# Spectral products of a long convolution: from paired half-array matmuls with the complex sum on VectorE to full 128x128 matmuls with the complex sum inside the inverse transform

## The chip, the cores and the metric

One core of a Trainium2 chip runs the whole program. The metric is the device time of one execution in microseconds (us); I quote medians. Engines are called as the profile calls them: PE is TensorE's matmul, PEld its weight load, DVE is VectorE, ACT is ScalarE, POOL is GpSimd, SP issues DMAs. The "granted clock" of a profile is the share of full TensorE clock that was granted.

## The reference, cut to what matters

There are two independent heads on 2048 positions and 576 channels. Head A is a dilated sliding-window attention. Head B multiplies shifted keys with values and convolves the result with a filter as long as the sequence; only this convolution is changed.

```python
def _B_ref(q, k, v, shift_k, ssm_k, ssm_D):
    ...                                        # kv = (k * 4-tap filter) * v
    kv_f = rfft(kv padded to 2S, float32)
    kf_f = rfft(ssm_k padded to 2S, float32)
    y_f = kv_f * kf_f                          # complex product per frequency and channel
    y = irfft(y_f)[:S].astype(bfloat16)
    y = y + kv * ssm_D
    return q * y
```

## The kernel before

The transform is split in two stages. Stage 1 writes its result to DRAM (`Dx` for the signal, `Dk` for the filter). Stage 2 is done in 8 steps i (two halves of the channels, four groups of 8 "h" columns): a **kernel transform** `kh_step(i)`, a **signal transform** `g_spec(i)`, the **product** `g_prod(i)` and the **inverse** `g_inv(i)`. These steps are interleaved with the attention's weighted sum over values, the **pv steps** tp = 0 to 7: `pv_mul` (DVE, tile `P`), `pv_sum` (PE, evicted by ACT into `xT`) and `pv_out`. Last, `y_step` does the final stage of the inverse.

```python
    def s2(Wt, g, dst, scale):                 # 64 columns per matmul: two h side by side in the array
        for prl in range(4):
            ps = psb()                         # 2 buffers of two PSUM banks
            for im in range(2):
                for hp in range(2):
                    nc.tensor.matmul(ps[64 * hp:64 * hp + 64, im, 0:HD],          # HD = 288
                                     W2[:, im, 8 * g + 2 * prl + hp].rearrange("p l f -> p (l f)"),
                                     Wt[:, 2 * prl + hp, :], start=True, stop=True, tile_position=(0, 64 * hp))
            nc.scalar.activation(dst[:, :, prl, :], ps[:, :, 0:HD], ACT.Copy, scale=scale)

    def g_prod(i):                             # 4 DVE instructions per step
        ...
        pin(nc.vector.tensor_tensor(m1[:], Xc[:], Kc[:, 0].unsqueeze(1).to_broadcast([128, 2, 4, HD]), ALU.mult))
        pin(nc.vector.tensor_tensor(m2, Xc[:], Kc[:, 1].unsqueeze(1).to_broadcast([128, 2, 4, HD]), ALU.mult))
        pin(nc.vector.tensor_tensor(m1[:, 0], m1[:, 0], m2[:, 1], ALU.subtract))
        pin(nc.vector.tensor_tensor(m1[:, 1], m1[:, 1], m2[:, 0], ALU.add))

    def g_inv(i):                              # 64 rows per matmul: two h above each other in the array
        ...
            for zi in range(2):
                for hp in range(2):
                    nc.tensor.matmul(ps[:, hp, 0:HD], IAt[64 * hp:64 * hp + 64, zi, 4 * g + prl, :],
                                     m1[64 * hp:64 * hp + 64, zi, prl, :], start=(zi == 0), stop=(zi == 1),
                                     tile_position=(64 * hp, 0))
            nc.scalar.activation(Y[:, 2 * prl:2 * prl + 2, :], ps[:, :, 0:HD], ACT.Copy)
        ...
    # k = kernel transform, g = signal step, y = last stage, per pv step tp
    plan = [(("k4", "g0"), ("k5", "g1")), (("k6", "g2"),), (("k7", "g3"), ("g4",)), (("g5",), ("y0",)),
            (("g6",), ("y1",), ("y2",)), (("g7",), ("y3",)), (("y4",), ("y5",)), (("y6",), ("y7",))]
    g_spec(0)
    for tp in range(8):
        pv_mul(tp)
        ...                                    # kh_step of the plan
        for n, i in enumerate(ng):
            if i + 1 < 8:
                g_spec(i + 1)
            if n == 0:
                pv_sum(tp)
            g_prod(i)
            if n == 0 and tp > 0:
                pv_out(tp - 1)
            g_inv(i)
        ...
```

`pin` keeps the DVE instructions of products and of `P` in program order. The order of everything else in an engine's queue is chosen when the program is built.

## Time and profile before

269.2 us (269.17, 269.21 and 271.84). The first part of the page gives busy time, share of the span and number of instructions of each engine:

```profile
span 268.5 us, 5519 instructions
PE 235.0 (88%) x2326; PEld 138.5 (52%) x2326; DVE 202.6 (75%) x216; ACT 163.4 (61%) x236; POOL 23.4 (9%) x59
```

The groups of instructions of the kernel before that the change touches. The columns are line, engine, operation, output <- inputs, shapes and count; then busy us and mean ns of one; then idle time just before them and what ended it:

```profile
L526 PE MATMUL psB<-Wt,W 128*64 128x288 bf16 x256 | 29.2, 311 | 7.1 <-ACT Xc L529 3.0
L529 ACT ACTIVATE Xc<-psB 128x576 bf16<-128x576 f32 x32 | 20.1, 649 | 3.4 <-PE psB L526 3.0
L529 ACT ACTIVATE Kc<-psB 128x576 bf16<-128x576 f32 x32 | 20.0, 650 | 2.2 <-PE psB L526 1.7
L568 DVE TENSOR_TENSOR m<-Xc,Kc 128x2304 bf16<-128x2304 bf16 x8 | 10.8, 1356 | 8.3 <-ACT Xc L529 7.3
L650 PEld LDWEIGHTS <-P 128*128 128x128 bf16 x512 | 30.0, 98 | 14.0 <-issue 8.6
```

The last of these is the weight load of the pv sums. It stood 8.6 us in "issue", that is, waiting for nothing that the profile shows. The timeline of the kernel before shows where (start us, length us, engine, line, what, how many, idle before):

```profile
187.48 0.44 PE L526 MATMUL psB<-Wt,W 128*64 128x288 bf16 x4
187.84 0.23 PEld L650 LDWEIGHTS <-P 128*128 128x128 bf16 x4 [0.23 <-issue]
187.84 0.40 PE L650 MATMUL psA<-ident,P 128*128 128x128 bf16 x4
188.17 0.14 PEld L526 LDWEIGHTS <-W 128*64 128x64 bf16 x4
188.17 0.44 PE L526 MATMUL psB<-Wt,W 128*64 128x288 bf16 x4
...
205.75 0.66 PE L581 MATMUL psB<-m,IAt 64*128 64x288 bf16 x8
...
210.71 0.42 PE L581 MATMUL psB<-m,IAt 64*128 64x288 bf16 x4
...
211.32 2.12 PE L666 MATMUL psA<-wv,xT 128*128 128x288 bf16 x16 [0.20 <-ACT xT L652]
```

Two things are to be read here. Each return from the half array (128\*64) to the full one (128\*128) shows an idle of 0.23 us ahead of the weight load. And the half-array matmuls run in pairs: 8 of L581 take 0.66 us and 4 take 0.42 us, so four more cost 0.24 us, 60 ns each. 16 full ones of the same 288 columns (L666) take 2.12 us, 130 ns each.

### The profile page before, as it was taken

The page shows a single profiled execution, that of the slowest core. Times are in us where ns is not written, and L with a number is a line of the kernel's source. Part 1 is how long each engine was busy: PE and PEld are TensorE (multiplying, and loading weights), DVE is VectorE, ACT ScalarE, POOL GpSimd, SP SyncE. Part 2 cuts the span into 40 slices and gives each one's busy share as a digit, 9 for nine tenths or more (in the row PEclk, how much of TensorE's full clock was granted, in tenths as well). Part 3 has the DMA queues.
Part 4 walks back from the last instruction along what each step waited for, and adds up shares of the span by engine and source line. Part 5 has one row for each costly group of instructions (what it writes and reads, how often), then busy time and mean ns, then how long its engine had stood idle before and what let it go on. Part 6 is the DMA issues. An engine that isn't in the chain of part 4 may idle for free.

```text
span 268.5 us, 5519 instructions
## 1 busy us (share of the span) xinstructions
PE 235.0 (88%) x2326; PEld 138.5 (52%) x2326; DVE 202.6 (75%) x216; ACT 163.4 (61%) x236; POOL 23.4 (9%) x59
## 2 busy tenths in 40 slices
PE   2999969999899999998997578898979998978793
PEld 2236344434366555464653247555645676847671
DVE  2599997999645576589986999879397668799431
ACT  2454448777736565858568895888867666251131
POOL 8200000000000000000068101000000010201200
PEclk9999999999999999999999989999997999999997
DMA  7996594785144352577276676464517576837945
GB/s 256 320 386 227 165 386 134 242 264 175 47 133 125 109 166 88 148 218 272 69 216 172 215 200 197 130 217 137 181 46 254 188 234 186 247 116 242 347 132 176
DMA packets 42544, 52.11 MB, mean 194 GB/s; under 512 B 2284, under 2 KB 35708, under 8 KB 42520
## 3 DMA queue, kind: packets, MB, share of 16 engines
q1 hardware_dynamic: 41190, 48.52, 55.7%
q0 software_dynamic: 1328, 3.25, 4.4%
q8 instruction: 18, 0.29, 0.5%
q14 instruction: 6, 0.05, 0.0%
q10 hardware_dynamic: 2, 0.00, 0.0%
HBM read 30.82 MB, written 18.87 MB: 185 GB/s over the span
## 4 chain that ended last, share of the span: by engine, by line
PE 56%; DVE 22%; ACT 11%; issue 4%; DMA 4%; POOL 2%; SPq 0%; ACTq 0%; DVEq 0%; POOLq 0%
PE psA L278 7%; PE psA L469 6%; PE psA L650 6%; PE psA L261 6%; PE psB L336 6%; PE psB L526 5%; DVE P L640 5%; PE psB L419 3%; PE psA L666 3%; DVE tA L375 3%; DMA Wt<-Dy 3%; DVE tB L370 2%; DVE m L568 2%; DVE sk L569 2%; ACT Xc L529 2%
## 5 line engine op out<-in xcount | busy, mean ns | idle before, releaser
L341 ACT ACTIVATE vst<-psB 128x768 bf16<-128x768 f32 x48 | 37.0, 812 | 12.7 <-PE psB L336 11.3
L466 DVE TENSOR_TENSOR wide<-q,k 128x2048 bf16<-128x2048 bf16 x32 | 38.9, 1228 | 7.4 <-PE psA L469 7.3
L640 DVE TENSOR_TENSOR P<-vX,vt 128x4608 bf16<-128x4608 bf16 x16 | 40.5, 2554 | 2.9 <-PE psA L656 2.8
L650 PE MATMUL psA<-ident,P 128*128 128x128 bf16 x512 | 37.7, 221 | 3.6 <-DVE P L640 2.9
L650 PEld LDWEIGHTS <-P 128*128 128x128 bf16 x512 | 30.0, 98 | 14.0 <-issue 8.6
L526 PE MATMUL psB<-Wt,W 128*64 128x288 bf16 x256 | 29.2, 311 | 7.1 <-ACT Xc L529 3.0
L278 PE MATMUL psA<-xT,wq 128*128 128x512 bf16 x128 | 34.4, 404 | 0.7 <-ACT xT L181 0.7
L469 PE MATMUL psA<-wide,Eh 128*32 128x256 bf16 x256 | 21.7, 400 | 1.1 <-ACT vX L266 1.1
L526 PEld LDWEIGHTS <-W 128*64 128x64 bf16 x256 | 12.9, 112 | 18.2 <-issue 14.9
L529 ACT ACTIVATE Xc<-psB 128x576 bf16<-128x576 f32 x32 | 20.1, 649 | 3.4 <-PE psB L526 3.0
L690 DVE TENSOR_TENSOR m<-psB,tA 128x576 bf16<-128x576 f32 x16 | 11.7, 755 | 13.8 <-PE psB L689 10.0
L584 ACT ACTIVATE tB<-psB 128x576 bf16<-128x576 f32 x32 | 19.4, 658 | 4.1 <-PE psB L581 3.0
L529 ACT ACTIVATE Kc<-psB 128x576 bf16<-128x576 f32 x32 | 20.0, 650 | 2.2 <-PE psB L526 1.7
L278 PEld LDWEIGHTS <-wq 128*128 128x128 bf16 x128 | 12.1, 101 | 16.2 <-issue 6.1
L261 PE MATMUL psA<-wv,xT 128*128 128x288 bf16 x128 | 19.9, 292 | 0.6 <-ACT vX L266 0.6
L629 POOL DMA_DIRECT2D wv<-in_A_wo_dram x18 | 8.9, 499 | 128.5 <-PE psA L261 127.3
L652 ACT ACTIVATE xT<-psA 128x1024 bf16<-128x1024 f32 x8 | 8.2, 1023 | 19.4 <-PE psA L650 19.4
L673 ACT ACTIVATE stageA<-psA 128x576 bf16<-128x576 f32 x16 | 9.5, 648 | 16.8 <-PE psA L670 11.6
L666 PE MATMUL psA<-wv,xT 128*128 128x288 bf16 x128 | 17.1, 286 | 2.0 <-ACT xT L652 2.0
L266 ACT ACTIVATE vX<-psA 128x576 bf16<-128x576 f32 x16 | 10.4, 650 | 12.4 <-PE psA L264 12.4
L261 PEld LDWEIGHTS <-xT 128*128 128x128 bf16 x128 | 15.6, 146 | 4.5 <-issue 3.6
L568 DVE TENSOR_TENSOR m<-Xc,Kc 128x2304 bf16<-128x2304 bf16 x8 | 10.8, 1356 | 8.3 <-ACT Xc L529 7.3
(126 smaller groups left out, 341.7 us busy)
## 6 DMA issues: line engine op xcount, KB each, us to landing
Dx<-vst SPq DMA_DIRECT2D x16, 288.0 KB, 3.0
Dk<-vst SPq DMA_DIRECT2D x16, 288.0 KB, 3.0
Wt<-Dk SPq DMA_DIRECT2D x8, 576.0 KB, 3.9
Wt<-Dx SPq DMA_DIRECT2D x8, 576.0 KB, 3.9
Dy<-tB SPq DMA_DIRECT2D x8, 576.0 KB, 2.7
Wt<-Dy SPq DMA_DIRECT2D x8, 576.0 KB, 5.5
wide<-in_B_k_dram SPq DMA_DIRECT2D x3, 1008.0 KB, 5.6
xnat<-in_A_x_dram SPq DMA_DIRECT2D x4, 576.0 KB, 8.7
```

Of the source, the lines that this page charges most:

```text
L261: nc.tensor.matmul(ps[:, di, 0:288], xTt[:, kb, t2, :], wv[:, kb, d0:d1], start=(kb == 0), stop=False)
L278: nc.tensor.matmul(ps[:, u, :], wcols(kb, comp, 2 * cp + u), xT[:, kb, t], start=(kb == 0), stop=False)
L341: nc.scalar.activation(vst[:, :, 384 * ch:384 * ch + 384], ps[:, :, 0:384], ACT.Copy)
L466: nc.vector.tensor_tensor(prod, qv, kv, ALU.mult)
L469: nc.tensor.matmul(psw[32 * j:32 * j + 32, u, 0:256].rearrange("p (a b) -> p a b", b=2), Eh[:, 2 * h + c, :], prod[:, c, :, 2 * j:2 * j + ...
L526: nc.tensor.matmul(ps[64 * hp:64 * hp + 64, im, 0:HD], W2[:, im, 8 * g + 2 * prl + hp].rearrange("p l f -> p (l f)"), Wt[:, 2 * prl + hp, ...
L529: nc.scalar.activation(dst[:, :, prl, :], ps[:, :, 0:HD], ACT.Copy, scale=scale)
L568: pin(nc.vector.tensor_tensor(m1[:], Xc[:], Kc[:, 0].unsqueeze(1).to_broadcast([128, 2, 4, HD]), ALU.mult))
L584: nc.scalar.activation(Y[:, 2 * prl:2 * prl + 2, :], ps[:, :, 0:HD], ACT.Copy)
L640: pin(nc.vector.tensor_tensor(P[:].rearrange("p w (d h) -> p w d h", h=H), vs, ath[t2 // 8][:, :, t2 % 2, (t2 % 8) // 2, :].unsqueeze(2).t ...
L650: nc.tensor.matmul(oacc[:, ct, 128 * u:128 * u + 128], Ps[u][:, wi, 128 * ct:128 * ct + 128], ident[:], start=(ct % 2 == 0 and u == 0 and ...
L666: nc.tensor.matmul(psos[u][:, di, 0:288], oT[:, ct, 2 * tp + u, :], wot[:, ct, d0:d1], start=(ct == 0), stop=False)
```

## The change

Intent: take the complex sums off DVE and use the whole array. A signal transform now computes, for each h, real over imaginary parts on the 128 partitions (64 + 64), and a second time imaginary over minus real. DVE multiplies both with the kernel's spectrum (real over minus imaginary), and the inverse transform, which now contracts over all 128 partitions, adds the parts up. The inverse's table is wider and is built later; the output stage gets a tile of its own. The core of the diff:

```diff
-    W2 = const.tile([128, 2, 32, 4, 16], BF16, name="W2")
-    IAt = const.tile([128, 2, 16, 128], BF16, name="IAt")
+    W2 = const.tile([128, 32, 3, 64], BF16, name="W2")        # cos-like, sin-like, minus cos-like
+    Msp = const.tile([128, 192], BF16, name="Msp")
+    ksg = const.tile([128, 1], FP32, name="ksg")              # +1/2048 over -1/2048
 ...
+    def inv_table(h4):
+        ps = psb()
+        for v in range(4):
+            for im in range(2):
+                nc.tensor.matmul(ps[64 * im:64 * im + 64, v // 2, 192 * (v % 2):192 * (v % 2) + 192],
+                                 W2[:, 4 * h4 + v, 0, :], Msp[:], start=True, stop=True, tile_position=(0, 64 * im))
+        nc.scalar.activation(IAts[0][:, 4 * h4:4 * h4 + 4, :]..., ps[:, :, 0:384], ACT.Copy)
 ...                                                            # kh_step: 8 full matmuls, 4 evictions, scale=ksg[:]
     def g_spec(i):
-        Xcs[i] = b2.tile([128, 2, 4, HD], BF16, name="Xc")
-        s2(Wxs[i], i % 4, Xcs[i], 1.0)
+        Xcs[i] = b2.tile([128, 8, 2, HD], BF16, name="Xc")
+        for hl in range(8):
+            h = 8 * (i % 4) + hl
+            ps = psb()
+            for v in range(2):
+                nc.tensor.matmul(ps[:, v, 0:HD], spec_cols(h, v), Wxs[i][:, hl, :], start=True, stop=True)
+            nc.scalar.activation(Xcs[i][:, hl], ps[:, :, 0:HD], ACT.Copy)
     def g_prod(i):
 ...                                                            # the four instructions above go
+        for q in range(2):
+            r = slice(4 * q, 4 * q + 4)
+            pin(nc.vector.tensor_tensor(Xc[:, r], Xc[:, r], Kc[:, r].unsqueeze(2).to_broadcast([128, 4, 2, HD]), ALU.mult))
     def g_inv(i):
 ...
+                for v in range(2):
+                    nc.tensor.matmul(ps[:, hp, 0:HD], IAts[0][:, 8 * g + hl, 64 - 64 * v:192 - 64 * v], Xcs[i][:, hl, v, :],
+                                     start=(v == 0), stop=(v == 1))
 ...
     g_spec(0)                                                  # plan unchanged
+            if i in (1, 2):
+                inv_table(2 * i + 2)
+                inv_table(2 * i + 3)
```

(Cut: three instead of four input buffers at the start, the building of `W2` with a third block, tables 0 to 3 built with the first four kernel transforms, the output stage's load split in two, buffers moved between pools.)

More of the change, by code (lines that the diff above doesn't have):

```diff
@@ L97 @@
     IB = const.tile([128, 2, 128], BF16, name="IB")
-    W2 = const.tile([128, 2, 32, 4, 16], BF16, name="W2")
-    IAt = const.tile([128, 2, 16, 128], BF16, name="IAt")
+    W2 = const.tile([128, 32, 3, 64], BF16, name="W2")
+    Msp = const.tile([128, 192], BF16, name="Msp")
+    ksg = const.tile([128, 1], FP32, name="ksg")
     Eh = const.tile([128, HC + 2, H], BF16, name="Eh")
     maskb = const.tile([128, 2, W, 2], BF16, name="maskb")
-    Db = const.tile([128, D], BF16, name="Db")
     vX = const.tile([128, 30, D], BF16, name="vX")
@@ L128 @@
     wq = wqp.tile([128, 5, 2 * D], BF16, name="wq")
-    xin = pool("xin", 4, "right")
-    xns = [xin.tile([128, 4, 640], BF16, name="xnat") for _ in range(4)]
+    xin = pool("xin", 3, "right")
+    xns = {}
     tw = pool("tw", 1, "right")
@@ L136, in load_x @@
     def load_x(qtr):
+        xns[qtr] = xin.tile([128, 4, 640], BF16, name="xnat")
         nc.sync.dma_start(xns[qtr][:, :, 0:D], xf[512 * qtr:512 * qtr + 512, :].rearrange("(sb p) c -> p sb c", p=128))
@@ L159 @@
     load_x(2)
-    load_x(3)
-    ones_f = tw.tile([128, 128], FP32, name="ones_f")
-    nc.gpsimd.memset(ones_f[:], 1.0)
     ident_f = tw.tile([128, 128], FP32, name="ident_f")
-    affine_pair(ident_f[:], ones_f[:], pattern=[[1, 128]], cm=-1, base_lo=0, base_hi_minus=0)
+    nc.gpsimd.memset(ident_f[:], 1.0)
+    affine_pair(ident_f[:], ident_f[:], pattern=[[1, 128]], cm=-1, base_lo=0, base_hi_minus=0)
     nc.vector.tensor_copy(ident[:], ident_f[:])
+    nc.gpsimd.memset(ksg[0:64, :], 1.0 / 2048)
+    nc.gpsimd.memset(ksg[64:128, :], -1.0 / 2048)
     def x_tr(qtr):
@@ L200 @@
     nc.scalar.activation(T1[:], n1[:], ACT.Sin, bias=pib[:], scale=-2.0 * np.pi / 512)
-    g2 = tw.tile([128, 32, 16], I32, name="g2")
-    nc.gpsimd.iota(g2[:], pattern=[[4, 32], [512, 16]], base=0, channel_multiplier=0)
+    n2 = tw.tile([128, 32, 3, 16], I32, name="n2")
+    nc.gpsimd.iota(n2[:, :, 2], pattern=[[4, 32], [512, 16]], base=0, channel_multiplier=0)
     sc_i = tw.tile([128, 4], I32, name="sc_i")
@@ L216 @@
     nc.vector.tensor_tensor(s0, s0, sc_f[:, 7:8], ALU.add)
-    n2 = tw.tile([128, 2, 32, 16], I32, name="n2")
-    nc.vector.tensor_scalar(n2[:, 0], g2[:], t2f, s0, op0=ALU.mult, op1=ALU.add)
-    nc.vector.tensor_scalar(n2[:, 1], n2[:, 0], 2048.0, None, op0=ALU.add)
+    nc.vector.tensor_scalar(n2[:, :, 0], n2[:, :, 2], t2f, s0, op0=ALU.mult, op1=ALU.add)
+    nc.vector.tensor_scalar(n2[:, :, 1], n2[:, :, 0], 2048.0, None, op0=ALU.add)
+    nc.vector.tensor_scalar(n2[:, :, 2], n2[:, :, 0], 4096.0, None, op0=ALU.add)
     nc.vector.tensor_single_scalar(n2[:], n2[:], 8191, ALU.bitwise_and)
-    C2 = tw.tile([128, 64, 16], BF16, name="C2")
-    nc.scalar.activation(C2[:].rearrange("p (i h) f -> p i h f", i=2), n2[:], ACT.Sin, bias=pib[:],
+    C2 = tw.tile([128, 96, 16], BF16, name="C2")
+    nc.scalar.activation(C2[:].rearrange("p (h i) f -> p h i f", i=3), n2[:], ACT.Sin, bias=pib[:],
                          scale=-2.0 * np.pi / 8192)
@@ L227 @@
     nc.vector.tensor_scalar(lmask[:], l_i[:], sc_f[:, 0:1], None, op0=ALU.is_equal)
-    nc.vector.tensor_tensor(W2[:].rearrange("p i h l f -> p (i h) l f"),
-                            C2[:].unsqueeze(2).to_broadcast([128, 64, 4, 16]),
-                            lmask[:].unsqueeze(1).to_broadcast([128, 64, 4, 16]), ALU.mult)
+    nc.vector.tensor_tensor(W2[:].rearrange("p h i (l f) -> p (h i) l f", l=4),
+                            C2[:].unsqueeze(2).to_broadcast([128, 96, 4, 16]),
+                            lmask[:].unsqueeze(1).to_broadcast([128, 96, 4, 16]), ALU.mult)
+    idr = ident[:].rearrange("p (a r b) -> p r a b", a=8, r=2)
+    mrs = Msp[:].rearrange("p (r a b) -> p r a b", r=3, a=8)
+    nc.vector.tensor_copy(mrs[:, 1:3], idr)
+    nc.vector.tensor_scalar(mrs[:, 0], idr[:, 1], -1.0, None, op0=ALU.mult)
     ones_e = tw.tile([128, HC + 2, H], FP32, name="ones_e")
@@ L311, in ia_tables @@
     def ia_tables():
-        for zi in range(2):
-            for p4 in range(2):
-                ptr = pb.tile([128, 2, 1024], BF16, name="psB")
-                for v in range(8):
-                    pr = 8 * p4 + v
-                    nc.tensor.transpose(ptr[:, v // 4, 128 * (v % 4):128 * (v % 4) + 128],
-                                        W2[:, zi, 2 * pr:2 * pr + 2].rearrange("p h l f -> p (h l f)"), ident[:])
-                nc.vector.tensor_copy(IAt[:, zi, 8 * p4:8 * p4 + 8, :].rearrange("p (a b) t -> p a (b t)", a=2), ptr[:, :, 0:512])
         ptr = pb.tile([128, 2, 1024], BF16, name="psB")
@@ L323, in ia_tables @@
         nc.vector.tensor_copy(IB[:], ptr[:, 0, 0:256].rearrange("p (a b) -> p a b", a=2))
-    vsts = {}
+    IAts = {}
+    def inv_table(h4):
[4 more added lines that the diff above has]
+                                 W2[:, 4 * h4 + v, 0, :], Msp[:], start=True, stop=True, tile_position=(0, 64 * im))
+        nc.scalar.activation(IAts[0][:, 4 * h4:4 * h4 + 4, :].rearrange("p (a b) t -> p a (b t)", a=2),
+                             ps[:, :, 0:384], ACT.Copy)
+    vsts, Dbs = {}, {}
     def s1_part(src, key, c2, ch, Dd, add_d):
@@ L338, in s1_part @@
                 n = 384 if ch == 0 else 192
-                nc.tensor.matmul(ps[:, ri, 0:n], row0[:], Db[:, 384 * ch:384 * ch + n], start=False, stop=True)
+                nc.tensor.matmul(ps[:, ri, 0:n], row0[:], Dbs[0][:, 384 * ch:384 * ch + n], start=False, stop=True)
         if True:
@@ L386 @@
     x_tr(0)
+    load_x(3)
     sk_step()
@@ L408 @@
         knats.append(kn)
+    Dbs[0] = Db = kpre.tile([128, D], BF16, name="Db")
     nc.gpsimd.dma_start(Db[:], B_ssm_D.partition_broadcast(128))
@@ L518, in at_step, with spec_cols @@
             nc.scalar.activation(ath[hf][:, 4 * u:4 * u + 4].rearrange("p w b j h -> p w b (j h)"), pst[:, u], ACT.Copy)
-    def s2(Wt, g, dst, scale):
-        for prl in range(4):
-            ps = psb()
-            for im in range(2):
-                for hp in range(2):
-                    nc.tensor.matmul(ps[64 * hp:64 * hp + 64, im, 0:HD],
-                                     W2[:, im, 8 * g + 2 * prl + hp].rearrange("p l f -> p (l f)"),
-                                     Wt[:, 2 * prl + hp, :], start=True, stop=True, tile_position=(0, 64 * hp))
-            nc.scalar.activation(dst[:, :, prl, :], ps[:, :, 0:HD], ACT.Copy, scale=scale)
+    def spec_cols(h, i0):
+        return W2[:, h, i0:i0 + 2, :].rearrange("p i m -> p (i m)")
     def load_wt(Dd, dh, g):
@@ L540, in kh_step @@
         Wt = load_wt(Dk, dh, g)
-        Kcs[i] = kf.tile([128, 2, 4, HD], BF16, name="Kc", bufs=6)
-        s2(Wt, g, Kcs[i], 1.0 / 2048)
+        Kcs[i] = kf.tile([128, 8, HD], BF16, name="Kc", bufs=6)
+        for prl in range(4):
+            ps = psb()
+            for hp in range(2):
+                nc.tensor.matmul(ps[:, hp, 0:HD], spec_cols(8 * g + 2 * prl + hp, 0), Wt[:, 2 * prl + hp, :],
+                                 start=True, stop=True)
+            nc.scalar.activation(Kcs[i][:, 2 * prl:2 * prl + 2, :], ps[:, :, 0:HD], ACT.Copy, scale=ksg[:])
     def pin(ins):
@@ L551, in pin @@
         return ins
-    Xcs, m1s, Wxs = {}, {}, {}
+    Xcs, Wxs = {}, {}
     def g_load(i):
@@ L560, in g_spec @@
             g_load(i)
-        Xcs[i] = b2.tile([128, 2, 4, HD], BF16, name="Xc")
-        s2(Wxs[i], i % 4, Xcs[i], 1.0)
+        Xcs[i] = b2.tile([128, 8, 2, HD], BF16, name="Xc")
+        for hl in range(8):
+            h = 8 * (i % 4) + hl
+            ps = psb()
+            for v in range(2):
+                nc.tensor.matmul(ps[:, v, 0:HD], spec_cols(h, v), Wxs[i][:, hl, :], start=True, stop=True)
+            nc.scalar.activation(Xcs[i][:, hl], ps[:, :, 0:HD], ACT.Copy)
     def g_prod(i):
         Xc, Kc = Xcs[i], Kcs[i]
-        m1 = m1s[i] = b2.tile([128, 2, 4, HD], BF16, name="m1")
-        m2 = slab("sk", 1, (2, 4, HD), "m2")
-        pin(nc.vector.tensor_tensor(m1[:], Xc[:], Kc[:, 0].unsqueeze(1).to_broadcast([128, 2, 4, HD]), ALU.mult))
-        pin(nc.vector.tensor_tensor(m2, Xc[:], Kc[:, 1].unsqueeze(1).to_broadcast([128, 2, 4, HD]), ALU.mult))
-        pin(nc.vector.tensor_tensor(m1[:, 0], m1[:, 0], m2[:, 1], ALU.subtract))
-        pin(nc.vector.tensor_tensor(m1[:, 1], m1[:, 1], m2[:, 0], ALU.add))
+        for q in range(2):
+            r = slice(4 * q, 4 * q + 4)
+            pin(nc.vector.tensor_tensor(Xc[:, r], Xc[:, r], Kc[:, r].unsqueeze(2).to_broadcast([128, 4, 2, HD]), ALU.mult))
     def g_inv(i):
         dh, g = i // 4, i % 4
-        m1 = m1s[i]
         Y = slab("tB", 1, (8, HD), "Y")
@@ L578, in g_inv @@
             ps = psb()
-            for zi in range(2):
-                for hp in range(2):
-                    nc.tensor.matmul(ps[:, hp, 0:HD], IAt[64 * hp:64 * hp + 64, zi, 4 * g + prl, :],
-                                     m1[64 * hp:64 * hp + 64, zi, prl, :], start=(zi == 0), stop=(zi == 1),
-                                     tile_position=(64 * hp, 0))
+            for hp in range(2):
+                hl = 2 * prl + hp
+                for v in range(2):
+                    nc.tensor.matmul(ps[:, hp, 0:HD], IAts[0][:, 8 * g + hl, 64 - 64 * v:192 - 64 * v], Xcs[i][:, hl, v, :],
+                                     start=(v == 0), stop=(v == 1))
             nc.scalar.activation(Y[:, 2 * prl:2 * prl + 2, :], ps[:, :, 0:HD], ACT.Copy)
@@ L612 @@
             kf = pool("kf", 1, "right")
+            IAts[0] = kf.tile([128, 32, 192], BF16, name="IAt")
             wk = pool("wk", 3, "right")
@@ L615 @@
             kh_step(n - 12)
+            inv_table(n - 12)
     with tc.high_priority():
@@ L679, in y_step @@
         Vw = wk.tile([128, 8, HD], BF16, name="Wt")
-        nc.sync.dma_start(Vw[:], by_f1(Dy, dh, 8 * c4, 8))
-        Vy = Vw[:].rearrange("p (c r t) d -> p c r t d", c=2, r=2)
+        Vy = Vw[:].rearrange("p (r t) d -> p r t d", r=2)
+        for r in range(2):
+            nc.sync.dma_start(Vy[:, r], by_f1(Dy, dh, 16 * r + 4 * c4, 4))
         qt = slab("tA", 2, (4, HD), "qt")
         nc.gpsimd.dma_start(qt, qb[:, 4 * c4:4 * c4 + 4, d0:d0 + HD])
-        stage = b2.tile([128, 2, 4, HD], BF16, name="m1")[:, 0]
+        stage = b2.tile([128, 4, HD], BF16, name="ystage")
         for u in range(2):
@@ L688, in y_step @@
                 for ri in range(2):
-                    nc.tensor.matmul(ps[:, v, 0:HD], IB[:, ri, :], Vy[:, u, ri, v, :], start=(ri == 0), stop=(ri == 1))
+                    nc.tensor.matmul(ps[:, v, 0:HD], IB[:, ri, :], Vy[:, ri, 2 * u + v, :], start=(ri == 0), stop=(ri == 1))
             (nc.vector.tensor_tensor(stage[:, 2 * u:2 * u + 2, :], ps[:, :, 0:HD], qt[:, 2 * u:2 * u + 2, :], ALU.mult))
-        nc.sync.dma_start(outb[:, 4 * c4:4 * c4 + 4, D + d0:D + d0 + HD], stage)
+        nc.sync.dma_start(outb[:, 4 * c4:4 * c4 + 4, D + d0:D + d0 + HD], stage[:])
     plan = [(("k4", "g0"), ("k5", "g1")), (("k6", "g2"),), (("k7", "g3"), ("g4",)), (("g5",), ("y0",)),
```

## The prediction

> **What bounds the kernel now.** No single engine does. The page's first table gives PE 88%, DVE 75%, ACT 61% of 268.5 us. By windows: in 146 to 164 us ACT is busy 15.6 of 18.0 us and PE 11.7; the timeline shows PE standing in the spectral matmuls (L526: 28 matmuls take 4.5 us) for ACT's evictions. In 164 to 245 us PE is busy 73.1 of 81.0, DVE 64.6, ACT 52.5: PE paces.
>
> **What changes, costed from the trace.**
>
> 1. PE. The half-array matmuls now run in concurrent pairs: on the timeline four more of L581 (64 rows) cost 0.23 us (0.65 against 0.42), about 58 ns each, while full 128x128 ones of the same 288 columns (L666, 16 in 2.12 us) cost 0.13 us each. L526 is alike. Kernel transforms go from 16 half to 8 full matmuls: equal. Signal transforms and the inverse keep 16 but full: about +1.0 us each, 8 times, +16 us in all. Against that stands the change of tile shape: L650 (full) between L526 groups starts and ends with a gap of some 0.12 us; between L650 and L689, both full, there is none. The Trainium skill, "TensorEngine Tiling (Array Packing)", Tiling Modes, says that changing the mode drains the array; this trace agrees. All-full matmuls save about 0.24 us per interleaved group, about 13 us (estimate). The new inverse table costs 8 x about 0.5 us, the removed transposes save 2.1. PE net: +3 to +6 us, nearly all in 164 to 245.
>
> 2. ACT. Signal transforms evict 8 instead of 4 tiles of 128x576 (649 ns each): +2.6 us x 8 = +21 us. The inverse table adds 8 evictions of 128x768 (812 ns): +6.5 us. ACT goes from 163 to about 191 us.
>
> 3. DVE. Products fall from 1.36+1.35+0.75+0.75 us to two of 1.35 us: -1.5 us x 8 = -12 us. The four table copies of 0.68 us go (-2.7); the 1.5 times larger table costs about +1.6. DVE ends near 190 us.
>
> 4. The output stage no longer shares m1 with the products: the wait of the product for the output DMA (1.1 us; the DMA is 2.4 us on the chain) goes.
>
> **How much is on the critical path.** 0 to 60 us: DVE and PE both slightly relieved, -1 us. 146 to 164 us: ACT paces, and gets two signal transforms (+5.2) and a table (+0.8): +4 us. 164 to 245: ACT 52.5 + about 16 + 3 = 71 of 81, PE 73 + about 4: both tight; DVE's 10 us help only where PE waits for it (about 5 us): +3 us. End: -1 us.
>
> **Prediction: 274 us, 265 to 283 eight times in ten. Faster by over 2%: 0.11; within: 0.43; slower: 0.46.**
>
> **What would show each step.** PE busy in matmul up by some us in the spectral and inverse groups, their "issue" gaps gone. Xc evictions 64 instead of 32, at 0.65 us. ACT about 190 us busy. Product group: 16 x 1.35 us. In 146 to 170 us the first pv sum (L650) starts later, at 166 to 169 instead of 164 us.
>
> **What would make it wrong.** If DVE really paced 164 to 245, its 10 us would show as a gain and the time would be 262 to 266. If the compiler's ordering lets pv matmuls fill the ACT-bound stretch at 150 to 164, the loss there vanishes. If it queues eight evictions before pv's own, each pv output waits up to 2.6 us more and the time exceeds 283. If the switch costs less than I read, PE grows by up to 16 us.

## More of the kernel before

To follow the time through the spectral stage I use the moments at which ACT evicts a pv sum into `xT`, once per pv step. The first, third and seventh of them in the kernel before:

```profile
167.79 1.02 ACT L652 ACTIVATE xT<-psA 128x1024 bf16<-128x1024 f32 x1 [1.61 <-PE psA L650]
...
193.74 1.02 ACT L652 ACTIVATE xT<-psA 128x1024 bf16<-128x1024 f32 x1 [1.07 <-PE psA L650]
...
245.16 1.02 ACT L652 ACTIVATE xT<-psA 128x1024 bf16<-128x1024 f32 x1 [4.85 <-PE psA L650]
```

The windows view of the kernel before gives busy time by stretch, cut at the third and the sixth of these evictions. The columns are window and length, then busy us and count of PE, PEld, DVE, ACT and POOL, then the granted clock, DMA share and GB/s:

```profile
146.50:193.70 47.20, 38.92 (x470) 24.71 (x468) 38.78 (x34) 39.21 (x62) 2.04 (x3) 0.96 0.58 186
193.70:233.30 39.60, 35.94 (x440) 25.08 (x442) 30.90 (x25) 23.89 (x41) 2.25 (x3) 0.96 0.57 183
```

In the first stretch ACT works 39.2 of 47.2 us, PE and DVE about as much. In the second PE is at 91% and ACT at 60%. ACT's load lies at the front of the stage.

## The result, and the profile after

284.26 us (283.67 to 284.42, 4 runs) against 269.51 us of before in the same comparison. The ratio is 1.052, with a 95% interval of 1.047 to 1.056. Here and below, a ratio is the one on record, over the fast runs of both kernels in the same rounds, so not quite the ratio of the medians that I quote. The change costs 14.8 us where I had said 4.8.

The first part of the page after:

```profile
span 282.6 us, 5493 instructions
PE 252.7 (89%) x2289; PEld 154.5 (55%) x2294; DVE 191.4 (68%) x199; ACT 188.8 (67%) x276; POOL 23.6 (8%) x61
```

The work is what I had counted: DVE 11 us less, ACT 25 us more. The groups of the kernel after that answer to those of before:

```profile
L573 PE MATMUL psB<-Wt,W 128*128 128x288 bf16 x128 | 28.1, 306 | 4.4 <-ACT Xc L574 3.0
L574 ACT ACTIVATE Xc<-psB 128x576 bf16<-128x576 f32 x64 | 38.2, 649 | 3.6 <-PE psB L573 3.2
L549 ACT ACTIVATE Kc<-psB,ksg 128x576 bf16<-128x576 f32 x32 | 21.6, 742 | 1.1 <-PE psB L547 0.8
L580 DVE TENSOR_TENSOR Xc<-Xc,Kc 128x2304 bf16<-128x2304 bf16 x16 | 21.4, 1356 | 23.1 <-ACT Xc L574 23.0
L660 PEld LDWEIGHTS <-P 128*128 128x128 bf16 x512 | 34.1, 97 | 4.6 <-DVE P L650 0.9
```

The 8.6 us of "issue" ahead of the pv sums' weight loads are gone: signal transform and pv sum are both full-array now. But the products wait 23 us for ACT's evictions, where they had waited 7.3 us. The Kc eviction became dearer, 742 against 650 ns, since its scale is a tile now.

The pv evictions after, the first, third and seventh:

```profile
171.96 1.02 ACT L662 ACTIVATE xT<-psA 128x1024 bf16<-128x1024 f32 x1
...
206.49 1.02 ACT L662 ACTIVATE xT<-psA 128x1024 bf16<-128x1024 f32 x1
...
258.73 1.02 ACT L662 ACTIVATE xT<-psA 128x1024 bf16<-128x1024 f32 x1 [3.53 <-PE psA L660]
```

The first two show no idle before them: ACT came to them straight from other work, whereas in before it had waited for PE. The windows after, cut at the same two pv steps:

```profile
146.50:206.50 60.00, 52.65 (x483) 35.56 (x483) 34.31 (x26) 55.18 (x89) 1.13 (x2) 0.86 0.44 143
206.50:248.50 42.00, 40.69 (x424) 30.56 (x425) 30.70 (x20) 29.94 (x53) 1.67 (x3) 1.00 0.53 170
```

From 146.5 us to the third pv eviction, ACT is now busy 55.2 of 60.0 us. The stretch has grown from 47.2 to 60.0 us: 12.8 of the 14.1 us that lie between the two profiles are there. (The granted clock in it, the third column from the right, is 0.86 against 0.96; more on this below.) Against the prediction, by subtraction of the eviction times (both profiles' last logit eviction is at 146.5 us, so the start gained nothing that lasted):

| stretch | before | after | difference | predicted |
|---|---|---|---|---|
| start to first pv eviction | 167.8 | 172.0 | +4.2 | -1 + 4 = +3 |
| first to seventh (my "164 to 245") | 77.4 | 86.8 | +9.4 | +3 |
| seventh to end of span | 23.3 | 23.9 | +0.5 | -1 |

The timeline of the kernel after shows the inside of the second pv step on ACT, with nothing between the pieces:

```profile
175.71 4.71 ACT L574 ACTIVATE Xc<-psB 128x576 bf16<-128x576 f32 x8
180.45 1.51 ACT L330 ACTIVATE IAt<-psB 128x768 bf16<-128x768 f32 x2
182.05 2.69 ACT L592 ACTIVATE tB<-psB 128x576 bf16<-128x576 f32 x4
184.64 2.63 ACT L549 ACTIVATE Kc<-psB,ksg 128x576 bf16<-128x576 f32 x4
187.14 5.01 ACT L574 ACTIVATE Xc<-psB 128x576 bf16<-128x576 f32 x8
192.05 1.02 ACT L662 ACTIVATE xT<-psA 128x1024 bf16<-128x1024 f32 x1
```

The second pv eviction stands behind sixteen signal evictions, a table, an inverse and a kernel transform.

### The profile page after: what moved, and what is told of

Its sections match the earlier page's. It is cut to its first block, busy times and chain, and to the rows that moved or that the text cites. A ratio compares the mean times of both kernels' runs of the same rounds, so it can differ in the third digit from the quotient of the medians.

```text
span 282.6 us, 5493 instructions
## 1 busy us (share of the span) xinstructions
PE 252.7 (89%) x2289; PEld 154.5 (55%) x2294; DVE 191.4 (68%) x199; ACT 188.8 (67%) x276; POOL 23.6 (8%) x61
## 4 chain that ended last, share of the span: by engine, by line
PE 60%; DVE 15%; ACT 13%; issue 5%; POOL 2%; DMA 2%; ACTq 0%; SPq 0%; DVEq 0%; POOLq 0%
PE psA L660 7%; PE psA L478 6%; PE psA L282 6%; PE psB L573 6%; PE psA L265 6%; PE psB L343 5%; ACT Xc L574 3%; DVE tA L382 3%; PE psB L428 3%; DVE P L650 3%; PE psB L547 3%; DVE tB L377 3%; PE psB L590 3%; DMA Wt<-Dy 2%; PE psA L676 2%
## 5 line engine op out<-in xcount | busy, mean ns | idle before, releaser
L574 ACT ACTIVATE Xc<-psB 128x576 bf16<-128x576 f32 x64 | 38.2, 649 | 3.6 <-PE psB L573 3.2
L660 PE MATMUL psA<-ident,P 128*128 128x128 bf16 x512 | 40.2, 219 | 0.3 <-DVE P L650 0.2
L580 DVE TENSOR_TENSOR Xc<-Xc,Kc 128x2304 bf16<-128x2304 bf16 x16 | 21.4, 1356 | 23.1 <-ACT Xc L574 23.0
L660 PEld LDWEIGHTS <-P 128*128 128x128 bf16 x512 | 34.1, 97 | 4.6 <-DVE P L650 0.9
L282 PE MATMUL psA<-xT,wq 128*128 128x512 bf16 x123 | 33.3, 398 | 1.0 <-ACT xT L181 0.7
L573 PE MATMUL psB<-Wt,W 128*128 128x288 bf16 x128 | 28.1, 306 | 4.4 <-ACT Xc L574 3.0
L549 ACT ACTIVATE Kc<-psB,ksg 128x576 bf16<-128x576 f32 x32 | 21.6, 742 | 1.1 <-PE psB L547 0.8
L590 PE MATMUL psB<-Xc,IAt 128*128 128x288 bf16 x128 | 19.1, 286 | 0.7 <-ACT tB L592 0.6
L683 ACT ACTIVATE stageA<-psA 128x576 bf16<-128x576 f32 x16 | 9.5, 648 | 14.1 <-PE psA L680 9.0
L701 DVE TENSOR_TENSOR ystage<-psB,tA 128x576 bf16<-128x576 f32 x16 | 11.6, 754 | 10.4 <-PE psB L700 10.2
L573 PEld LDWEIGHTS <-W 128*128 128x128 bf16 x128 | 12.1, 102 | 11.8 <-issue 8.1
```

Of the source, the lines that this page charges most:

```text
L282: nc.tensor.matmul(ps[:, u, :], wcols(kb, comp, 2 * cp + u), xT[:, kb, t], start=(kb == 0), stop=False)
L549: nc.scalar.activation(Kcs[i][:, 2 * prl:2 * prl + 2, :], ps[:, :, 0:HD], ACT.Copy, scale=ksg[:])
L573: nc.tensor.matmul(ps[:, v, 0:HD], spec_cols(h, v), Wxs[i][:, hl, :], start=True, stop=True)
L574: nc.scalar.activation(Xcs[i][:, hl], ps[:, :, 0:HD], ACT.Copy)
L590: nc.tensor.matmul(ps[:, hp, 0:HD], IAts[0][:, 8 * g + hl, 64 - 64 * v:192 - 64 * v], Xcs[i][:, hl, v, :], start=(v == 0), stop=(v == 1))
L660: nc.tensor.matmul(oacc[:, ct, 128 * u:128 * u + 128], Ps[u][:, wi, 128 * ct:128 * ct + 128], ident[:], start=(ct % 2 == 0 and u == 0 and ...
```

## The experiments

Theories: **E**, ACT's doubled evictions are the loss. **M**, the full-array matmuls are: their PE busy time grew by 17.7 us. **O**, only the order in ACT's queue is. **B**, E and M each cost most of it alone. Where the result is wrong I say so; the comparison with the reference reported all runs as correct, those too, so it does not see this fault. Every run was timed in 3 rounds beside the kernel before (medians 269.1 to 270.3 us). The five batches ran on four different chips, and the kernel after was not timed again beside them, so a difference from after's 284.3 us is one between two comparisons; there the ratios to before are the safer guide. A "dose" is work that I add on purpose to see what it costs.

### First batch: doses

**e1. Half of the signal evictions on DVE** (on after).

```diff
-            nc.scalar.activation(Xcs[i][:, hl], ps[:, :, 0:HD], ACT.Copy)
+            if hl % 2 == 0:
+                nc.scalar.activation(Xcs[i][:, hl], ps[:, :, 0:HD], ACT.Copy)
+            else:
+                nc.vector.tensor_copy(Xcs[i][:, hl], ps[:, :, 0:HD])
```

> Kernel after, but 4 of the 8 signal-transform evictions of each step go to DVE (which is busy only 12 of 20 us in 160 to 240 us); PE work is unchanged. Theory E (eviction: ACT is full from 146 to 207 us and paces there): ACT falls by 32 x 0.65 = 21 us, the time falls from 284 by 7 to 12 us, to 272 to 277. Theory M (the full-array matmuls pace; PE is 17.7 us busier): stays within 282 to 286. Theory O (only the order of ACT's queue hurts): falls by 4 to 8, since fewer evictions stand ahead of the pv one.

Measured: 287.2 us, ratio 1.065, above every range. That speaks against E as I had put it, but the experiment was not clean: what ACT no longer did waited elsewhere. DVE's evictions (0.75 us each) stand in its own queue between instructions of 2.55 us, and each holds one of two PSUM buffers. ACT then waited 14.3 us for signal matmuls (3.2 us in after).

**e2. Evictions twice, on before.**

```diff
-            nc.scalar.activation(dst[:, :, prl, :], ps[:, :, 0:HD], ACT.Copy, scale=scale)
+            for _ in range(times):                                  # 2 for the signal
+                nc.scalar.activation(dst[:, :, prl, :], ps[:, :, 0:HD], ACT.Copy, scale=scale)
```

> Kernel before, every signal-transform eviction done twice (same values, right result): 32 more ACT instructions of 0.65 us, +21 us of ACT, as in after; PE, DVE work unchanged. Theory E: 269.5 rises to 276 to 283. Theory M: stays within 268 to 272. Theory O: rises as under E, since these too stand in the queue ahead of the pv eviction.

Measured: 278.8 us, ratio 1.034. E's (and O's) range; M is wrong as the only cause. Evictions alone, with no new matmul, cost 9 us. The granted clock was lower with them, 0.95 to 0.97 in the four runs against 0.97 to 0.99, and how much of the 9 us that is was not separated.

**e3. Half-array matmuls twice, on before.**

```diff
-            for im in range(2):                                     # signal transforms
+            for im in [0, 1] * times:                               # 2 for the signal
 ...
-            for zi in range(2):                                     # inverse
+            for zi in [0, 1, 0, 1]:
```

> Kernel before, the half-array matmuls of the signal transforms and of the inverse issued twice (right result): 256 more matmuls of about 58 ns, +15 us of PE occupancy, the same as I estimate for going from half to full arrays; ACT and DVE unchanged. Theory M: 269.5 rises by 8 to 15 us. Theory E: rises by 2 to 5 us. Theory O: by 0 to 3.

Measured: 285.5 us, ratio 1.058: the full 15 us. So PE does pace the kernel before, as the prediction said, though not alone (e2), and E is wrong as the only possible cause. This dose is not what the change does, though: it keeps the half arrays and their switching.

**e4. pv sum ahead of the next signal transform, on after.**

```diff
-            if i + 1 < 8:
-                g_spec(i + 1)
             if n == 0:
                 pv_sum(tp)
+            if i + 1 < 8:
+                g_spec(i + 1)
```

> Kernel after with pv_sum put before the next signal transform in program order, so that the pv eviction goes ahead of the eight Xc evictions in ACT's queue; all work unchanged. Theory O: falls by 5 to 10 us. Theory E: -2 to +1, since ACT has as much to do in 146 to 207 us, and the products then wait for what pv no longer waits for. Theory M: -1 to +1.

Measured: 285.3 us, ratio 1.056. The pv evictions did come earlier (the second at 189.8 instead of 192.1 us), and the end did not. O is refuted as the cause of the loss.

### Second batch: taking parts out of after

**e5. All matmuls, half the evictions** (wrong result: of each pair the matmul v = 1 goes first and v = 0 overwrites it in PSUM; each product works on half the columns and is done twice).

```diff
-        for hl in range(8): ...                                     # 8 tiles, 8 evictions
+        for prl in range(4):
+            ps = psb()
+            for hp in range(2):
+                hl = 2 * prl + hp
+                for v in (1, 0):
+                    nc.tensor.matmul(ps[:, hp, 0:HD], spec_cols(8 * (i % 4) + hl, v), Wxs[i][:, hl, :], start=True, stop=True)
+            nc.scalar.activation(Xcs[i][:, 2 * prl:2 * prl + 2], ps[:, :, 0:HD], ACT.Copy)
 ...                                                            # cut: product, inverse
```

> Kernel after, wrong result on purpose: all its matmuls stay (16 full ones per signal transform, 16 per inverse), but each step evicts 4 tiles as before did, not 8; product time about the same (4 x 0.75 us against 2 x 1.36). ACT falls by 21 us. Theory E (ACT's evictions are the loss): falls from 284 to 271 to 276. Theory M (the full matmuls are the loss): stays within 280 to 285. Theory B (each alone costs most of it, since they alternate on two PSUM buffers): falls by 2 to 7 only.

**e6. All evictions, half the matmuls** (wrong result: one matmul, its PSUM read twice; the inverse takes only v = 0).

```diff
-            for v in range(2):
-                nc.tensor.matmul(ps[:, v, 0:HD], spec_cols(h, v), ...)
-            nc.scalar.activation(Xcs[i][:, hl], ps[:, :, 0:HD], ACT.Copy)
+            nc.tensor.matmul(ps[:, 0, 0:HD], spec_cols(h, 0), ...)
+            nc.scalar.activation(Xcs[i][:, hl], ps[:, 0:1, 0:HD].to_broadcast([128, 2, HD]), ACT.Copy)
```

> Kernel after, wrong result on purpose: all evictions stay (8 of 128x576 per signal transform), but only 8 of 16 matmuls in each signal transform and 8 of 16 in each inverse: about 16 us less of PE. Theory M: falls to 268 to 273. Theory E: stays within 280 to 284. Theory B: 276 to 281, near the kernel before with its evictions doubled (278.8).

**e7. Both halved** (e5 with one matmul per h in the signal transform and in the inverse; wrong result).

> Kernel after with both taken out (8 matmuls and 4 evictions per signal transform, 8 matmuls per inverse), wrong result on purpose. What is left of the change is the inverse table, the dearer Kc eviction (742 against 650 ns), the separate output tile and the shorter products. If those do little, 263 to 269, all theories alike; above 271, something else than matmuls and evictions is a cause of its own.

**e8. Both doses of e2 and e3, on before.**

> Kernel before with both doses: matmuls of signal transforms and inverse twice, and signal evictions twice. Alone the doses cost 9.1 us (evictions) and 15.2 us (matmuls) here. If additive (two separate critical parts): 292 to 296. If one hides behind the other (theory B, the same stretches are waited out once): 284 to 289.

Measured, as a square (medians, us; ratio to before):

| on after | all matmuls | half of them |
|---|---|---|
| all evictions | 284.3 (1.052) | 281.6 (1.043), e6 |
| half of them | 274.7 (1.019), e5 | 267.2 (0.990), e7 |

e5 is in E's range; e6 is in E's too, and just above B's. e7 is 1% faster than before (interval 0.984 to 0.996). In e6 the granted clock was lower, 0.94 to 0.96 against 0.97 to 0.98 in after, which may hide part of what its fewer matmuls save. Without the doubled evictions the change costs 5.4 us; with them it costs 15. Halving the matmuls alone gives back 2.6 us, and 7.5 us once the evictions are out of the way. On before, e8 took 292.0 us (1.083), at the lower edge of "additive": 22.8 us for doses of 9 and 15. Theory B holds only in part: the two overlap somewhat in after, hardly in before. In e5's profile the first pv eviction is at 167.6 us, where before has it, and first to seventh takes 80.5 us, 3.1 us more than before:

```profile
167.59 1.02 ACT L664 ACTIVATE xT<-psA 128x1024 bf16<-128x1024 f32 x1 [1.21 <-PE psA L662]
...
248.10 1.03 ACT L664 ACTIVATE xT<-psA 128x1024 bf16<-128x1024 f32 x1 [3.53 <-PE psA L662]
```

The page of e5 has one more lesson:

```profile
span 272.0 us, 5472 instructions
PE 244.3 (90%) x2294; PEld 152.5 (56%) x2294; DVE 193.1 (71%) x215; ACT 172.6 (63%) x244; POOL 23.6 (9%) x61
```

The matmul program is that of after (2294 weight loads in both), and still PE is "busy" 8.4 us less than after. Of these, 4.6 us lie between the first and the seventh pv eviction (83.0 against 78.4 us of busy time in 888 matmuls each, both at a granted clock of 1.00), so matmuls that stand among more evictions show as busy for longer. 3.9 us lie in 146.5 us to the first pv eviction, where the granted clock differed too (0.66 in after, 0.84 in e5). The Trainium skill, "Trainium Kernel Development and Optimization", Performance Expectations, calls matmul busy time a bad metric for how close a kernel is to roofline, because matmuls are pipelined. This pair of profiles agrees that it is a poor measure; that pipelining is the reason they do not show.

### Third batch: is it crowding?

**e9. The sign moved from the Kc eviction into the table, on after** (scale a constant again).

```diff
-            nc.scalar.activation(Kcs[i][:, 2 * prl:2 * prl + 2, :], ps[:, :, 0:HD], ACT.Copy, scale=ksg[:])
+            nc.scalar.activation(Kcs[i][:, 2 * prl:2 * prl + 2, :], ps[:, :, 0:HD], ACT.Copy, scale=1.0 / 2048)
 ...
-                                 W2[:, 4 * h4 + v, 0, :], Msp[:], ...
+                                 W2[:, 4 * h4 + v, 0, :], (Msn if im else Msp)[:], ...       # Msn = -Msp
```

> Kernel after, right result; the sign of the imaginary rows moves from the Kc eviction (whose scale was a tile: 742 ns each) into the inverse table (scale a constant again: 650 ns expected). Takes 32 x 0.09 = 3 us off ACT, 16 of these 32 in the packed stretch 146 to 200 us. If ACT paces there: falls from 284.3 by 1 to 3 us. If matmuls pace: by under 0.7.

Measured: 282.8 us, but a ratio of 1.051 against 1.052 of after. The third pv eviction came 1.2 us earlier (205.3 us). Inconclusive: 1.5 us by the medians, 0.2 us by the ratios. The Kc eviction itself was back at 654 ns.

**e12. The last four kernel transforms one to two pv steps later, on after.**

```diff
-    plan = [(("k4", "g0"), ("k5", "g1")), (("k6", "g2"),), (("k7", "g3"), ("g4",)), (("g5",), ("y0",)),
-            (("g6",), ("y1",), ("y2",)), (("g7",), ("y3",)), ...
+    plan = [(("g0",), ("g1",)), (("k4", "g2"),), (("k5", "g3"), ("g4",)), (("k6", "g5"), ("y0",)),
+            (("k7", "g6"), ("y1",), ("y2",)), (("g7",), ("y3",)), ...
```

> Kernel after, right result; the last four kernel transforms go one to two pv steps later (k4 with g2, k5 with g3, k6 with g5, k7 with g6), out of the stretch where ACT is 18 of 20 us busy; all work the same. If what I missed was the crowding of ACT early in the stage (its total of 71 of 81 us hid it), this gets back 2 to 5 us: 279 to 282. If PE's total work paces: 283.5 to 285.

Measured: 286.8 us, ratio 1.066, slower, and above both ranges. By the third pv eviction it was 2.4 us ahead (204.1 us), as the crowding theory wants; by the fifth it was 1.7 us behind. What leaves the packed stretch is paid in the next one.

**e13. The same plan on before, with the output tile of its own.**

> Kernel before, right result, with the spread plan of e12 and the output stage's own tile (as in after). The separate tile should save about 1 us (waits for the output DMA), the spreading 1 to 3 us where ACT held PE at 150 to 162 us: 265.5 to 268.5. If neither is on the critical path: 269 to 270.

Measured: 274.3 us, ratio 1.017 (1.012 to 1.021), slower, and above both ranges; the two edits were not tried apart. In before, the kernel transforms k4 and k5 had run at 150 to 163 us, where PE had room; later they had not. Neither hoped-for gain appeared.

**e10. Signal spectrum computed once, its halves swapped by DMA.**

```diff
 ...
+                nc.tensor.matmul(ps[:, hp, 0:HD], spec_cols(8 * (i % 4) + hl, 0), Wxs[i][:, hl, :], start=True, stop=True)
+            nc.scalar.activation(Xc[:, 0, 2 * prl:2 * prl + 2], ps[:, :, 0:HD], ACT.Copy)
+        nc.sync.dma_start(Xc[0:64, 1], Xc[64:128, 0])
+        nc.sync.dma_start(Xc[64:128, 1], Xc[0:64, 0])
 ...                                                            # cut: table, product, inverse, plan
```

> A version of after that keeps the full-array form without the doubled work, right result: the signal transform computes real over imaginary once (8 full matmuls, 4 evictions), and two DMAs within SBUF swap the halves of partitions; constant scale; inverse table of 256 columns (eviction about 1.02 us); kernel transforms spread as in e12 (five Kc buffers). ACT -21 us, PE -8 us against after. From e5 (274.7) and e7 (267.2): 268 to 272 if the DMA's latency hides; above 275 if the products now wait for the swap.

Measured: 277.6 and 278.0 us in the two fast runs, ratio 1.032. The other two, 284.1 and 284.2 us, are slow ones, and the profiled run is one of them. So the fast runs are above the 275 us that I had named for products that wait, and 8.6 us above before; still, this is the fastest version of after that gives the right result. In the slow profile a swap took 5.5 us to land (median) and the products waited 28.4 us for swaps; there is no profile of a fast run, so that this wait is the loss is not shown.

### Fourth batch: table and DVE's order

**e14. Every inverse table built twice, on after.**

```diff
-            inv_table(n - 12)
+            inv_table(n - 12)
+            inv_table(n - 12)                                       # and so the four later ones
```

> Kernel after, right result, every inverse table built twice: 8 more evictions of 0.81 us and 64 more matmuls. If the table is a good part of the 5.4 us that e5 leaves: rises by 3 to 5 us. If it is nearly free: by 0 to 1.5, and the 5.4 is the full-array matmuls.

Measured: 292.0 us, ratio 1.084: 7.7 us more than after, above both ranges. The profile shows how most of it adds up. Window to the third pv eviction:

```profile
146.50:213.40 66.90, 59.20 (x547) 39.17 (x547) 34.05 (x26) 62.60 (x98) 1.73 (x3) 0.85 0.42 132
```

The third pv eviction is at 213.4 us, 6.9 us later than in after. Seven of the eight added table evictions stand in this window, 5.7 us, and ACT is busy 62.6 of 66.9 us, 7.4 us more than in after. A table added in this stretch, eviction and matmuls together, is paid in full.

**e15. `P` of the next pv step ahead of the product on DVE, on after.**

```diff
             if n == 0:
                 pv_sum(tp)
+                if tp < 7:
+                    pv_mul(tp + 1)                                  # and not at the head of the loop
```

> Kernel after, right result; on DVE the weighted values P of the next pv step come before the product of this one, so they no longer wait behind it (in after the products wait 23 us for evictions). If DVE's order carries the loss: falls by 4 to 9 us. If ACT's and PE's throughput carries it (PE waits for P only 0.2 us in after): within -1.5 to +1.5.

Measured: 292.2 us, ratio 1.085: worse by 8, outside both ranges. DVE now waited 41 us for the pv sums to free a `P` buffer (13.5 us in after, both between 146 and 250 us), with the products behind it. That speaks for the products, not `P`, as what the rest waits for: signal eviction, product, inverse, next pv step.

**e18. The DMA swap of e10 with `P` first and kernel transforms a step earlier.**

> As e10 (swap by DMA, half the evictions and signal matmuls), right result, with P ahead of the product as in e15 and kernel transforms k4 to k7 one step earlier than in e10. If e10 lost by products that wait for the swap and hold up P: 268 to 274. If the wait itself is on the path (product, inverse, output): 276 to 281.

Measured: 283.3 us, ratio 1.052, all four runs fast: above both ranges, and 5.5 us slower than the fast runs of e10. The products waited 8.2 us for swaps, and DVE 25.7 us for `P` buffers.

**e17. `P` first, on before, with the output tile of its own.**

> Kernel before, right result, with P ahead of the product and the output stage's own tile. PE waits for P 2.9 us in the pv sums of before, and for the output DMA's tile about 1 us: 265.5 to 268.5 if those are on the path; 269 to 270 if not.

Measured: 274.7 us, ratio 1.022 (1.015 to 1.029), slower, above both ranges. As in e15, DVE now waited for the pv sums to free `P` buffers, 17.6 us against 2.8 us in before.

### Fifth batch: load off ACT, once more

**e20. Table evictions on DVE and constant scale, on after.**

```diff
-        nc.scalar.activation(IAts[0][:, 4 * h4:4 * h4 + 4, :]..., ps[:, :, 0:384], ACT.Copy)
+        nc.vector.tensor_copy(IAts[0][:, 4 * h4:4 * h4 + 4, :]..., ps[:, :, 0:384])
```

> Kernel after, right result, with the constant Kc scale of e9 and the inverse table's 8 evictions on DVE (which is idle more than half of 165 to 205 us). Takes 6.5 + 3 us off ACT, 8 of it before 207 us. If ACT paces one for one there: the third pv eviction comes at 198 to 201 us instead of 206.5, the time falls from 284.3 to 276 to 280. If DVE's queue holds the PSUM buffer instead, as in e1: 282 to 286.

Measured: 285.2 us, ratio 1.059: no gain, though ACT has 7.8 us less to do. The queues were also ordered anew: the softmax's exponential ran at 158.7 instead of 153.4 us, and the second pv eviction came at 183.4 us, 8.6 us earlier than in after, with the third at 206.3 us, no earlier. The time is in the range that I had named for DVE's queue holding the PSUM buffer, which the run does not prove. It refutes the simple form "every eviction taken off ACT is won".

**e21. e5 with the edit of e20** (wrong result).

> As e5 (4 evictions per signal transform, all matmuls, wrong result on purpose) with the constant scale and the table's evictions on DVE: ACT now no busier than in before. What remains over 269.2 is the price of full-array matmuls less the gain of the products. If the 5.4 us that e5 leaves were table and scale: 269 to 271.5. If full matmuls: 273 to 275.

Measured: 278.1 us, ratio 1.031: slower than e5, above both ranges. It does not split the 5.4 us: moving the table to DVE costs something of its own (0.95 us each there, in a queue in which products and `P` stand). The pv evictions show where: first to seventh takes 79.3 us, 1.9 us more than before, but the first comes at 172.0 us, as late as in after, though ACT has no more work than in before (163.7 us over the span).

No version that gives the right result beat the kernel before. e7 (267.2 us) did, by 1%, but computes half of the sums.

## Why the prediction was wrong

**What bounds the kernel before.** "In 164 to 245 us ... PE paces" held as far as it went: 15 us of added matmuls cost 15 us (e3). But evictions were not free there either: 21 us of them cost 9 us (e2).

**PE.** "PE net: +3 to +6 us, nearly all in 164 to 245" agrees with the runs as far as they go. e5 has all the new matmuls and before's number of signal evictions, and takes 3.1 us more than before between the first and the seventh pv eviction. The "issue" gaps of the pv weight loads, 8.6 us, are gone, as the step on tile shapes said. Those of the spectral matmuls' own loads are not: 14.9 us in before, 8.1 + 8.0 us after, where they stand beside waits for evictions. The rise of PE busy time by 17.7 us is no measure of work, as e5 shows. That the 3.1 us are the matmuls is not shown, since e5 has the new table, scale and products too.

**DVE and ACT totals.** DVE 191 us ("near 190"), ACT 189 us ("about 191"), products 16 x 1356 ns, 64 signal evictions of 649 ns: as predicted. The Kc eviction was overlooked; see below.

**146 to 164 us.** "ACT paces ... +4 us": the first pv eviction is 4.2 us late, and on time in e5. The first pv sum starts at 166.2 us ("166 to 169"). The number was right; whether for the reason given stays open. From 146.5 us to the first pv eviction the granted clock was 0.92 in before, 0.66 in after and 0.84 in e5 (in 150 to 165 us 0.89, 0.50 and 0.77), and e21 was as late with no more ACT work than before. In 160 to 165 us (1.00 before, 0.50 after) the 16 transposes of the second softmax half took 1.91 us in after, 1.07 us in before. What the evictions and what the clock cost in this stretch was not separated.

**The step that failed** is "164 to 245: ACT 52.5 + about 16 + 3 = 71 of 81, PE 73 + about 4: both tight; DVE's 10 us help only where PE waits for it (about 5 us): +3 us." The mechanism, ACT's doubled evictions, had been named; its price in this stage was mis-sized. I took 71 of 81 us as room. It measured +9.4 us: 3.1 us are there without the doubled evictions (e5), 6.3 us come with them. Together with the 4.4 us ahead of the first pv eviction (172.0 against 167.6 us) these make up the 10.6 us between the profiled runs of after and e5 (9.6 us by the medians). The clock is no rival here: between the first and the seventh pv eviction it was 1.00 in after and in e5, 0.98 in before. Of the +9.4 us, 8.6 lie between the first and the third. The windows there of before, after and e5 (same columns as above):

```profile
167.79:193.74 25.95, 23.97 (x304) 14.76 (x304) 18.29 (x13) 21.83 (x37) 0.00 (x0) 1.00 0.51 172
171.96:206.49 34.53, 32.24 (x341) 23.15 (x340) 17.84 (x10) 32.71 (x54) 0.00 (x0) 1.00 0.44 147
167.59:197.69 30.10, 28.99 (x328) 22.59 (x329) 18.14 (x16) 26.38 (x42) 0.00 (x0) 1.00 0.46 152
```

ACT is busy 84% in before, 95% in after, 88% in e5. About half of the 8.6 us, 4.4, goes with the doubled evictions; 4.2 are there in e5 too, which gains 1.0 after the third. The average hid that ACT's work is not spread evenly: to the third pv eviction ACT already had 39.2 of 47.2 us of work in before, 8 us of room. The change added some 16 us there (55.2 us measured). In that stretch a table more is paid in full (e14), and even before the change doubled signal evictions cost 9 us (e2). But ACT is not the only limit there: e20 took 6.2 us off it between 146.5 us and the third pv eviction, and that eviction came no earlier. In the profile's chain of the work that ended last, ACT and PE take turns in after: mostly ACT from 172.0 to 178.2 us and again from 187.9 to 193.1 us, mostly PE between and from there to 205.9 us.

**The condition I had named** ("If it queues eight evictions before pv's own, each pv output waits up to 2.6 us more and the time exceeds 283") came true word for word in the queue, and was still not the cause: e4 removed it and won nothing. All of the queue's work had still to be done before the next product, which would explain it; e4 shows only that the order did not matter.

**The output tile and the split load** show no gain at the end of the kernel (+0.5 us instead of -1).

**What stays open.** Of the 5.4 us that remain without the doubled evictions, the share of table, scale and full matmuls was not settled: e14 says that a second table is dear in the packed stretch, e20 and e21 that moving the table to DVE does not win it back. That the kernel's queues are ordered anew at each edit, and by how many us this alone can move the time, was not measured; with it, differences of 2 to 3 us between these variants are not to be explained one by one.

## What to carry to other kernels

When a change moves work from a busy engine to one with room, look for the room in the stretch where the work will stand, not in the average over the stage: here 61% over the span and 65% over the stage were 83% in the first 47 us. Count evictions as part of a matmul's price: a form that makes each matmul's output distinct (imaginary over minus real, computed again) doubles what has to leave PSUM, and the 1.5 us of DVE work saved per step were worth less than that here. Moving evictions to another engine with a full queue won nothing here (e1, e20): look at who then holds the PSUM buffers. And look at the granted clock beside the busy times, and at the state of each run before quoting a median (e10).

## What the Trainium skill lacked or had wrong

- "TensorEngine Tiling (Array Packing)", Tiling Modes, says that a change of tiling mode drains the array, but not what it costs. Here the idle ahead of the pv sums' weight loads, on the return to the full array, was 0.24 us in the mean (8.6 us in 36 cases, before), and none of it is left where the signal transform is full-array too (after).
- The same page, PSUM Bottleneck, advises, for tiled matmuls, to use both ScalarE and VectorE for evictions. It does not say what else VectorE's queue may hold. Here, with full-array signal matmuls, two PSUM buffers and instructions of 2.55 us in that queue, it did not help: 287.2 us with half of the signal evictions there, 284.3 us without (e1), and no gain with the table's (e20).
- Not lacking, but overlooked by me: "ScalarE: Activation LUTs", What ACT_TABLE_LOAD costs, gives about 93 ns for each per-partition pointer operand. The scale tile cost 92 ns (742 against 650 ns), in 32 evictions.
